# Fetching the condition vector c through the GpSimd queue in a fused adaLN transformer block

## Chip, cores and metric

The kernel runs on one core of a Trainium2 chip. The metric is the device time of one execution in microseconds. Three runs of the kernel before gave 560.43, 561.49 and 562.05 us, a median of 561.49 us.

## What is computed

A transformer block on x of 2048 rows by 512. A condition vector c of 512 numbers is turned into six modulation vectors by one product with w_mod (512 x 3072). The reference, cut to what matters:

```python
x = A_x
mod = (_silu(c) @ w_mod).reshape(c.shape[0], 6, 1, -1)
sa, ca, ga, sb, cb, gb = (mod[:, i] for i in range(6))
h = _layernorm(x) * (1 + ca) + sa
x = x + ga * attention(h)      # 32 heads on 8 kv heads, last 512 keys of the cache
h = _layernorm(x) * (1 + cb) + sb
x = x + gb * mlp(h)            # 512 -> 1792, relu, -> 512
```

Nothing of the attention can start before the first modulation: h needs the shift sa and the scale ca, which need silu(c) and the first third of w_mod (columns 0 to 1023, 1 MB).

## The kernel before

The 2048 rows are four blocks of 512, and each block with each of 32 heads is one unit, 128 in all. For each unit TensorE makes q from the normalised and modulated block (hT) and the head's columns of wq, then scores against the keys, then the product with the values; ScalarE takes the exponential between the two. The output projection and the second half run in the gaps and at the end. All instructions are written in program order into one stream for each engine; a helper (`kb.op`) works out which semaphores each instruction waits for. So the order on an engine is the order in which the build function calls it, and a DMA stands in the stream of the engine that issues it. `dma` takes SyncE unless it is given another engine.

The change touches the start, where the first block is made ready. What happens there, with the lines of the profile:

- Two DMAs bring the first block of x, one half from SyncE, one from ScalarE (L1559). Then c comes as 4 rows of 256 bytes from SyncE (L1560). The modulation weights of sa and ca come in two halves along the contracted dimension, `load_wm01(0)` from SyncE and `load_wm01(1)` from ScalarE (L1561, L1562). After them come wq of heads 0 and 1 from ScalarE, and from SyncE wq of heads 2 and 3, the first keys (a transposing DMA) and the first values. In the profile all plain DMAs carry the line of the helper, L1303, and all transposing ones L1302; one tells them apart by the tile. The weights' tile is called wmw.
- GpSimd makes constants (L1567 to L1575): a tile of ones, the identity matrix by an affine select (L1569), and some memsets.
- TensorE runs 7 products on the tile of ones whose result isn't used (`warm`, L1378, shown as L1371), then turns c into a column by a transpose with the identity (L1415), then 9 more of those products.
- ScalarE takes exp(-c) and a copy of c (L1416, L1417); GpSimd makes silu(c) of them in three steps (L1420 to L1422), the second of which is a power.
- Layer norm of x, four tiles of 128 rows: DVE makes the statistics (L1381, L1382) of tiles 0 to 2, ScalarE those of tile 3. GpSimd takes the power -0.5 of the variances in two steps (L1590), the first for tiles 0 and 1, the second for tiles 2 and 3. DVE normalises tiles 0 to 2 (L1392), and GpSimd tile 3 (L1603).
- TensorE makes the modulation: 32 products of one column each (wmw with silu(c)), 16 with the half that SyncE fetched, then the transposes of tile 0 (L1374), 16 with the other half, and the transposes of tiles 1, 2 and 3. DVE adds the ones for the scale (L1437, modc).
- DVE and ScalarE apply scale and shift to the transposed tiles (L1623 and L1625), half a block at a time, and TensorE makes q of units 0 and 1 from the halves.

The order of TensorE's stream there, as the code has it (L1605 to L1638):

```python
    for f in fs[:len(fs) // 2]:
        f()
    ln_tposes(0, TB[0])
    for f in fs[len(fs) // 2:]:
        f()
    ...
    for tl in range(1, TPB):
        ln_tposes(tl, TB[tl // 2])
    ...
    q_half(0, 0, CC_ORDER, QBK)
```

Of the kernel before, what the change touches and what calls it, by code (L numbers as in the profile page):

```python
# [1198 lines left out]
def build_fast(nc, es, top, A_x, A_k_cache, A_v_cache, A_wq, A_wo, B_x, B_w1, B_w2, c, w_mod, out, flag):  # L1199
    P = 128  # L1200
# [27 lines left out]
    def T(name, shape, dt=BF):  # L1228
        return es.enter_context(nc.sbuf_tensor(name, shape, dt))
# [27 lines left out]
    c_row = T("c_row", [DC, P])  # L1257
# [33 lines left out]
    POOL = kb.stream("pool", sem("s_pool"))  # L1291
    SP = kb.stream("sp", sem("s_sp"))

    def dsem(key):
        if key not in kb.dma_cnt:
            kb.add_dma_sem(key, sem("d_" + key))
        return key

    def dma(out_ap, in_ap, key, reads=(), writes=(), transpose=False, eng=None):
        k = dsem(key)  # L1300
        if transpose:
            return kb.op(SP, lambda e: e.dma_start_transpose(out_ap, in_ap), reads=reads, writes=writes, dma_sem=k)  # L1302
        return kb.op(eng or SP, lambda e: e.dma_start(out_ap, in_ap), reads=reads, writes=writes, dma_sem=k)  # L1303
# [10 lines left out]
    R_ident, R_ones, R_c, R_sc, R_scf, R_tmp, R_cst = (Res(n) for n in ("ident", "ones", "c", "sc", "scf", "tmp", "cst"))  # L1314
# [34 lines left out]
    def load_wm01(i, eng=None):  # L1349
        c0, c1 = i * DC // 2, (i + 1) * DC // 2  # L1350
        dma(wm01[:, c0:c1, :], wm01v[:, c0:c1, :], f"wm{i}", writes=[R_wm[i]], eng=eng)
# [205 lines left out]

    for i in range(2):
        dma(x_sb[:, 2 * i:2 * i + 2, :], xv[:, 2 * i:2 * i + 2, :], f"xa{i}", writes=R_x[2 * i:2 * i + 2], eng=ACT if i else SP)  # L1559
    dma(c_row[:, :], c[0].rearrange("(c p) -> c p", p=P), "c", writes=[R_c])  # L1560
    load_wm01(0)  # L1561
    load_wm01(1, ACT)  # L1562
    load_wq(0, 2, ACT)
# [4 lines left out]
    kb.op(POOL, lambda e: e.memset(cst[:, 0:1], -0.5), writes=[R_cst])  # L1568
    kb.op(POOL, lambda e: e.affine_select(ident[:, :], ones[:, :], pattern=[[1, P]], compare_op=ALU.is_equal, fill=0.0,  # L1569
                                          base=0, channel_multiplier=-1), reads=[R_ones], writes=[R_ident])  # L1570
    kb.op(POOL, lambda e: e.memset(cst[:, 1:2], eps), writes=[R_eps])
    kb.op(POOL, lambda e: e.memset(cst[:, 3:4], -1.0), writes=[R_eps])
    kb.op(POOL, lambda e: e.memset(v_sb[:, :, :, P:VW], 1.0), writes=[R_v1])
# [217 lines left out]
def bass_adaLN_cond__sliding_block_cached__dense_activation_relu__prompt_kernel(  # L1791
# [14 lines left out]
    with ExitStack() as top:  # L1806
        flag = top.enter_context(nc.sbuf_tensor("flag", [1, 8], mybir.dt.int32))
        with ExitStack() as es:
            kb, fast, cut, dma_cnt, flag_ev = build_fast(nc, es, top, *args, flag)
            sems = dict(kb.sems)  # L1810
            meet = top.enter_context(nc.semaphore("s_meet"))
# [71 lines left out]
```

## Time and profile before

| what | us |
|---|---|
| median of three runs | 561.49 |
| the profiled execution, its own time | 560.62 |
| its span, first to last instruction | 558.9 |
| TensorE busy (4060 products) | 549.8 |
| GpSimd busy (53 instructions) | 54.8 |
| c: issue on SyncE, start and duration | 1.24, 0.36 |
| wmw from SyncE: issue to landing | 6.3 |
| wmw from ScalarE: issue to landing | 5.0 |
| TensorE's wait for wmw before its first modulation product | 0.48 |
| TensorE's wait for c | 0.28 |

Times inside the span count from its first instruction. A product's duration is the time of its passage; products follow each other faster than that, so their durations overlap. The engine called POOL in the profile is GpSimd, SP is SyncE, ACT is ScalarE, DVE is VectorE, PE is TensorE and PEld its weight loads. An entry of SPq or ACTq is a DMA being issued. The start, up to the first score product at 12.79 us, is the part in which TensorE is not busy all the time.

### The profile page before, as it was taken

The numbers are of one execution on the slowest core, as the hardware profiler recorded it, in microseconds if no ns is written. First come the engines' busy times: TensorE is split into PE (matmuls) and PEld (weight loads), VectorE is DVE, ScalarE is ACT, GpSimd is POOL, SyncE is SP. The second block draws the span as 40 slices with busy tenths as digits, with TensorE's granted clock in tenths as the row PEclk, the third lists the DMA queues.
The fourth block names the chain that finished last, engine by engine and source line by source line (L and its number), as shares of the span: only waits on it lengthen the run. The fifth ranks groups of instructions, "written<-read, shape, count | busy, mean of one in ns | idle before, by whom it ended". The sixth has DMA issues, their size and how long they took to land.

```text
span 558.9 us, 9664 instructions
## 1 busy us (share of the span) xinstructions
PE 549.8 (98%) x4060; PEld 315.6 (56%) x4134; DVE 252.9 (45%) x549; ACT 349.4 (63%) x453; POOL 54.8 (10%) x53
## 2 busy tenths in 40 slices
PE   8999999999999999999999999999999999999998
PEld 4665555555555555555555555555555654444444
DVE  4455555553546544335445443333354438322134
ACT  5986666666666666666666666666666644432500
POOL 3000022004400000033000000332000000000000
PEclk9999999999999999999999999999999999999999
DMA  9997663522115144352352412111214110200001
GB/s 267 260 206 175 140 154 55 114 42 73 40 38 76 39 79 111 58 133 57 94 95 57 76 39 39 39 39 38 39 39 76 39 30 0 47 30 23 21 30 47
DMA packets 113309, 42.67 MB, mean 76 GB/s; under 512 B 93928, under 2 KB 112104, under 8 KB 113256
## 3 DMA queue, kind: packets, MB, share of 16 engines
q1 hardware_dynamic: 112024, 40.82, 34.4%
q10 hardware_dynamic: 1232, 1.15, 0.6%
q8 instruction: 33, 0.54, 0.4%
q14 instruction: 20, 0.16, 0.1%
HBM read 18.35 MB, written 2.10 MB: 37 GB/s over the span
## 4 chain that ended last, share of the span: by engine, by line
PE 97%; DMA 1%; issue 1%; SPq 0%; ACT 0%; DVE 0%
PE psS L1371 28%; PE psO L1371 27%; PE psQ L1371 23%; PE psW L1371 19%; DMA wmw<-in_w_mod_dram 1%; PE psS L1374 0%; SPq L1303 0%; ACT qT L1484 0%; DVE PT L1713 0%; DVE PT L1715 0%; PE psO L1374 0%
## 5 line engine op out<-in xcount | busy, mean ns | idle before, releaser
L1492 ACT ACTIVATE PT<-psS 128x1024 bf16<-128x1024 f32 x256 | 262.6, 1028 | 127.2 <-PE psS L1371 127.2
L1371 PE MATMUL psS<-qT,kT 128*128 128x512 bf16 x508 | 150.9, 379 | 0.7 <-ACT qT L1484 0.6
L1371 PEld LDWEIGHTS psO<-v,PT 128*128 128x128 bf16 x2048 | 126.6, 98 | 30.2
L1371 PE MATMUL psO<-v,PT 128*128 128x129 bf16 x2048 | 137.0, 220 | 0.0
L1371 PE MATMUL psQ<-hT,wq 128*128 128x512 bf16 (+1 forms) x510 | 130.5, 377 | 0.2
L1502 DVE RECIPROCAL rinv<-psO 128x4 f32<-128x4 f32 x128 | 23.4, 182 | 229.0 <-PE psO L1371 229.0
L1371 PE MATMUL psW<-wo,oT 128*128 128x512 bf16 x454 | 118.1, 379 | 3.0
L1503 DVE TENSOR_TENSOR o<-psO,rinv 128x512 bf16<-128x512 f32 x128 | 88.5, 691 | 4.4
L1371 PEld LDWEIGHTS psQ<-hT,wq 128*128 128x128 bf16 x512 | 50.0, 98 | 60.1 <-ACT qT L1484 0.4
L1371 PEld LDWEIGHTS psS<-qT,kT 128*128 128x128 bf16 x512 | 49.5, 98 | 59.1 <-ACT PT L1492 0.7
L1484 ACT ACTIVATE qT<-psQ 128x512 bf16<-128x512 f32 x127 | 75.2, 592 | 0.8 <-PE psQ L1371 0.8
L1702 ACT ACTIVATE wq<-psS 128x512 bf16<-128x512 f32 x56 | 33.4, 597 | 49.4 <-PE psS L1371 48.9
L1371 PEld LDWEIGHTS psW<-wo,oT 128*128 128x128 bf16 x512 | 45.0, 98 | 32.9 <-DVE acc L1525 1.2
L1525 DVE TENSOR_TENSOR acc<-psW,acc 128x512 f32<-128x512 f32 x48 | 33.2, 692 | 6.7 <-PE psW L1371 6.7
L1371 PE MATMUL psO<-wmw,wq 128*128 128x512 bf16 (+1 forms) x165 | 32.8, 352 | 0.3
L1528 POOL TENSOR_TENSOR acc<-acc,gaf 128x512 f32<-128x512 f32 x12 | 15.6, 1303 | 146.9 <-DVE acc L1525 139.8
L1387 POOL TENSOR_TENSOR rstd<-rstd,cst 128x4 f32<-128x4 f32 x7 | 7.2, 1027 | 216.1 <-DVE rstd L1386 216.1
L1713 DVE TENSOR_TENSOR PT<-psO,gbf 128x512 f32<-128x512 f32 (+1 forms) x12 | 7.5, 624 | 40.4 <-PE psO L1371 40.4
L1371 PE MATMUL psS<-h2T,wmw 128*128 128x512 bf16 x109 | 25.0, 379 | 0.2
L1371 PEld LDWEIGHTS psO<-wmw,wq 128*128 128x128 bf16 x168 | 15.3, 98 | 16.5
L1371 PE MATMUL psS<-hT,wmw 128*128 128x512 bf16 x110 | 24.4, 379 | 0.1
L1381 DVE BATCH_NORM_STATS2 st<-x 128x6 f32<-128x512 bf16 x31 | 21.1, 680 | 4.8 <-DMA x<-in_A_x_dram 4.8
(82 smaller groups left out, 190.9 us busy)
## 6 DMA issues: line engine op xcount, KB each, us to landing
wo<-in_A_wo_dram SPq DMA_DIRECT2D x4, 1024.0 KB, 5.9
wq<-in_A_wq_dram SPq DMA_DIRECT2D x7, 512.0 KB, 5.0
wmw<-in_B_w_dram SPq DMA_DIRECT2D x14, 256.0 KB, 3.1
wmw<-in_w_mod_dram SPq DMA_DIRECT2D x5, 512.0 KB, 5.0
oT<-o SPq DMA_TRANSPOSE x128, 2.4
out_dram<-PT SPq DMA_DIRECT2D x15, 128.0 KB, 1.7
x<-in_A_x_dram SPq DMA_DIRECT2D x3, 512.0 KB, 4.4
v<-in_A_v_cache_dram SPq DMA_DIRECT2D x8, 128.0 KB, 4.1
```

The source lines that it names most:

```text
L1371: kb.op(PE, lambda e: e.matmul(out_ap, lhsT, rhs, start=start, stop=stop), reads=reads, group_writes=[R_b[k] for k in bk], signal=signal)
L1381: kb.op(DVE, lambda e: e.bn_stats(st[:, t, :], x_sb[:, t, :]), reads=[R_x[t]], writes=[R_st[t]])
L1387: kb.op(POOL, lambda e: e.tensor_tensor(rstd[:, sl], rstd[:, sl], cst[:, 0:1].to_broadcast([P, hi - lo]), op=ALU.pow), reads=R_rstd[sl] + ...
L1484: kb.op(ACT, lambda e: e.activation(qT[u % NQT][:, :], bank[bk], ACTF.Copy), reads=[R_b[bk]], writes=[R_qT[u % NQT]])
L1492: kb.op(ACT, lambda e: e.activation(PT[u % NPT][:, pr * 2:pr * 2 + 2, :], s_ps[pr][:, :, :], ACTF.Exp, scale=scale), reads=[R_b[pr * 2], R ...
L1502: kb.op(DVE, lambda e: e.reciprocal(rinv[:, u, :], o_ps[:, :, P]), reads=[R_b[5], R_b[6]], writes=[R_rinv])
L1503: kb.op(DVE, lambda e: e.tensor_tensor(o_sb[u % NOS][:, :, :], o_ps[:, :, 0:P], rinv[:, u, :].unsqueeze(2).to_broadcast([P, TPB, P]), op=A ...
L1525: kb.op(DVE, lambda e: e.tensor_tensor(acc[:, tl, :], bank[WBK], acc[:, tl, :], op=ALU.add), reads=[R_b[WBK], R_acc[tl]], writes=[R_acc[tl]])
L1528: kb.op(eng, lambda e: e.tensor_tensor(acc[:, tl, :], acc[:, tl, :], gaf[:, :], op=ALU.mult), reads=[R_acc[tl], R_ga], writes=[R_acc[tl]])
L1702: kb.op(ACT, lambda e: e.activation(h1T[b % 2][:, fc, :], bank[bk], ACTF.Relu), reads=[R_b[bk]], writes=[R_h1[b % 2][fc]], pre=all_events( ...
L1713: kb.op(DVE, lambda e: e.tensor_tensor(yt[i][:, c0:c1], bank[bk][:, c0:c1], gbf[:, c0:c1], op=ALU.mult), reads=[R_b[bk], R_gb], writes=[R_ ...
```

## The change

The DMA that fetches c is moved from SyncE's stream, where it stood second, to GpSimd's stream, after the affine select that makes the identity and before the memsets of the constants. On SyncE the first half of the modulation weights follows the half of x directly. What c is used for, and all waits on it, are the same.

```diff
     for i in range(2):
         dma(x_sb[:, 2 * i:2 * i + 2, :], xv[:, 2 * i:2 * i + 2, :], f"xa{i}", writes=R_x[2 * i:2 * i + 2], eng=ACT if i else SP)
-    dma(c_row[:, :], c[0].rearrange("(c p) -> c p", p=P), "c", writes=[R_c])
     load_wm01(0)
     load_wm01(1, ACT)
     load_wq(0, 2, ACT)
...
     kb.op(POOL, lambda e: e.memset(cst[:, 0:1], -0.5), writes=[R_cst])
     kb.op(POOL, lambda e: e.affine_select(ident[:, :], ones[:, :], pattern=[[1, P]], compare_op=ALU.is_equal, fill=0.0,
                                           base=0, channel_multiplier=-1), reads=[R_ones], writes=[R_ident])
+    dma(c_row[:, :], c[0].rearrange("(c p) -> c p", p=P), "c", writes=[R_c], eng=POOL)
     kb.op(POOL, lambda e: e.memset(cst[:, 1:2], eps), writes=[R_eps])
     kb.op(POOL, lambda e: e.memset(cst[:, 3:4], -1.0), writes=[R_eps])
     kb.op(POOL, lambda e: e.memset(v_sb[:, :, :, P:VW], 1.0), writes=[R_v1])
```

## The prediction

> **What bounds the kernel now.** I read four views in this order: the page, the chain of waits from 0 to 30 us, the timeline of the first 16 us, and the DMA queues in half-microsecond windows. The page says where a microsecond counts at all:
>
> ```profile
> PE 549.8 (98%) x4060; PEld 315.6 (56%) x4134; DVE 252.9 (45%) x549; ACT 349.4 (63%) x453; POOL 54.8 (10%) x53
> PE 97%; DMA 1%; issue 1%; SPq 0%; ACT 0%; DVE 0%
> PE psS L1371 28%; PE psO L1371 27%; PE psQ L1371 23%; PE psW L1371 19%; DMA wmw<-in_w_mod_dram 1%; PE psS L1374 0%; SPq L1303 0%; ACT qT L1484 0%; DVE PT L1713 0%; DVE PT L1715 0%; PE psO L1374 0%
> ```
>
> TensorE is the bound, and it has no pause worth naming after the start. So the change can only move the start, and what it moves there passes to the end one to one, until TensorE is in its steady loop. The 1% of DMA is one transfer at the start, the first half of the modulation weights (chain of waits):
>
> ```profile
> 1.66 6.31 DMA wmw<-in_w_mod_dram
> 7.97 0.14 issue
> 8.11 0.54 PE psQ L1371 x16
> ```
>
> That transfer is the third that SyncE issues; c is the second. Timeline of the first 16 us (start, duration, engine, line, what; in brackets the idle time before it and who ended that):
>
> ```profile
> 1.23 0.46 ACTq L1303 DMA_DIRECT2D wmw<-in_w_mod_dram  x1
> 1.24 0.36 SPq L1303 DMA_DIRECT2D c_row<-in_c_dram  x1
> 1.32 0.29 POOL L1569 TENSOR_SCALAR_AFFINE_SELECT ident<-ones 128x128 bf16<-128x128 bf16 x1 [0.30 <-POOL cst L1568]
> 1.66 0.41 SPq L1303 DMA_DIRECT2D wmw<-in_w_mod_dram  x1
> 4.49 0.18 PE L1415 MATMUL psO<-ident,c_row 4*128 4x4 bf16 x1 [0.28 <-DMA c_row<-in_c_dram]
> 6.47 0.20 POOL L1422 TENSOR_TENSOR sc_bf<-c_f,tmp 128x4 bf16<-128x4 f32 x1
> 6.79 0.70 POOL L1590 TENSOR_TENSOR rstd<-rstd,cst 128x2 f32<-128x2 f32 x1
> 7.79 0.80 POOL L1590 TENSOR_TENSOR rstd<-rstd,cst 128x2 f32<-128x2 f32 x1 [0.30 <-DVE rstd L1587]
> 8.62 0.41 DVE L1392 TENSOR_SCALAR xn<-x,mv,rstd 128x512 bf16<-128x512 bf16 x1 [0.27 <-POOL rstd L1590]
> 8.69 0.90 POOL L1603 TENSOR_SCALAR xn<-x,s,rstd 128x512 bf16<-128x512 bf16 x1
> 9.65 0.34 PE L1374 MATMUL psS<-ident,xn 128*128 128x128 bf16 x3
> 10.11 0.35 PEld L1371 LDWEIGHTS psQ<-hT,wq 128*128 128x128 bf16 x3 [0.24 <-issue]
> 10.64 0.10 PEld L1371 LDWEIGHTS psQ<-hT,wq 128*128 128x128 bf16 x1 [0.17 <-ACT hT L1625]
> ```
>
> The reader is to see a second path here, which the chain doesn't print because it follows one releaser only. GpSimd makes the last tile of the normalised x (L1603), which ends at 8.69 + 0.90 = 9.59; the transposes of that tile begin on TensorE at 9.65; and they stand on TensorE ahead of the first q product (10.11). This path comes from x through DVE and GpSimd and holds no modulation weight. The two paths meet within half a microsecond.
>
> The queues show why the weights are late (q1 is SyncE's, q10 is ScalarE's; packets, MB, share of 16 engines), first from 4 to 4.5 us, then from 5 to 5.5:
>
> ```profile
> q10 hardware_dynamic: 95, 0.19, 99.5%
> q1 hardware_dynamic: 5, 0.01, 3.4%
> ...
> q1 hardware_dynamic: 73, 0.15, 77.4%
> q10 hardware_dynamic: 25, 0.04, 20.6%
> ```
>
> From 3.5 to 5 us SyncE's queue moves next to nothing while ScalarE's half, issued 0.43 us earlier, has the engines; then they change over. x's two halves, issued at the same 0.79 us, share them evenly. So the order of issue decides the order of transfer, and 0.42 us of issue time can be worth that much or more of landing.
>
> **What the Trainium skill says.** "DMA: Bandwidth & Descriptors", section "SWDGE vs HWDGE vs iDMA": a DMA issued from GpSimd has its descriptors computed by GpSimd's own cores, and its packets go to the same 16 engines, which take turns between its queue and the hardware queues. The trace of before has no such DMA, only q1, q10 and instruction queues, so it can't confirm that. Same page, "Why a DMA increments its semaphore by 16 and not by 1": from GpSimd all 16 engines post the completion whatever the shape, so c, which is 4 rows of 256 bytes, would wait for the slowest engine of a loaded set. "SBUF — State Buffer", section "SBUF: two separate sides": GpSimd can't write descriptors while some DVE operations hold the shared port. The trace rules that out here: DVE's first operation starts at 4.80 us. "TensorE: Matmul & The Clock Gate", Part 1: the array starts at half clock and needs a busy window of about 3.4 us. The trace agrees that there is such a step: the filler products of L1378 follow each other every 0.43 us up to 6.29 and every 0.22 from 6.60.
>
> **The change part by part.** (1) SyncE loses c's issue: 1.66 - 1.24 = 0.42 us. Everything behind it moves up by that: these weights to about 1.24, two wq heads (2.11), the first key transpose (2.62) and value rows (4.49). The weights now start level with ScalarE's half (1.23), so I expect the two halves to share the engines as x's halves do. What gets in ahead of them today is part of ScalarE's wq, which q10 carries beside them from 5.5 us to their end near 6.75: by the windows 0.03 + 0.05 + half of 0.09 = 0.125 MB, at 0.37 MB per us 0.34 us. Bounds for the gain: 0 if SyncE's half still queues behind ScalarE's, 0.5 if both halves (1.05 MB at 0.38 MB/us from 3.5 us, plus the 1.1 us that x's halves take from last byte to landing) land at 7.4. I take 0.34: landing at 7.63, first modulation product at 7.77. ScalarE's half moves from 1.23 + 5.0 = 6.2 to about 7.5, and its products (8.73, then 8.39) still find it. wq, needed at 10.11, shares with the other two heads' wq, which land by 2.11 + 7.2 = 9.3: covered by 0.8 us. The key transpose and value rows are needed after 12.5 and only come earlier.
>
> (2) GpSimd gains one issue between L1569, which ends at 1.61, and the memsets of L1571 to L1575. The queue behind it is five memsets (0.7 us from 1.57 to 2.27), then L1420, which waits for c anyway and runs at 4.98. With 1.0 us for the descriptors (same page, "Latency and other measured facts") the memsets end at 3.3: covered by 1.7 us. The eps column is read by ScalarE at 6.82, the ones of v after 16 us, the zeros and ones of m01 at 9.30.
>
> (3) c lands at another time. Before: used at 4.49. The nearest row is that DMA itself, 3.25 us from issue to use under this load; the page's section on the anatomy of a GpSimd DMA prices the whole at 2.0 us. Lower bound: 1.61 + 2.0 = 3.6, no gain, as the seven filler products hold TensorE to 4.0 and DVE's statistics wait for x until 4.80. Upper bound: 1.61 + 1.0 + (3.25 - 0.36) = 5.5. I take 4.6, a tenth late. That shifts L1420 to L1422 and the first power (L1590, 6.79 to 7.49) by 0.1. The second power starts at 7.79 by DVE's word, 0.30 after the first's end, of which some 0.1 is GpSimd's own step: 0.2 us of delay is free. On TensorE the nine fillers end at 7.63 + 0.1, before 7.77.
>
> (4) What the earlier weights buy. modc (9.30) would start 0.34 earlier, but DVE is in L1392 until 8.62 + 0.41 = 9.03: 0.24 earlier. ScalarE's first shift-and-scale (9.57) and with it its second (L1625) move by that, and the wait of 0.17 us at 10.64 goes. What is late next: the transposes of the last tile stay at 9.65, held by GpSimd's 9.59, so the first q product stays at 10.11 and the fourth can't come before 10.11 + 3 x 0.11 = 10.44. So only 0.17 us comes out at the end; the other 0.17 of the 0.34 is idle time.
>
> Sum: 560.62 (the profiled execution: span 558.9 and 1.7 around it) - 0.17 = 560.45. That execution lies 0.87 below the median of 561.49, so in terms of medians 561.3. A measurement of this kernel can tell some 0.3% (1.7 us) from no change; ten times the gain.
>
> **The rivals.** A: the gain is nothing, 561.5: the halves still run one after the other, or x's path through L1603 is alone decisive. For it: 9.65 follows 9.59 at once. Against it: the 0.17 wait on ScalarE is recorded. B, on the other side: c comes late from GpSimd. Its place is the order on GpSimd: L1420 to L1422 stand ahead of both powers and of L1603, so each 0.1 us of c beyond 4.7 ends at the last tile, its transposes and every q product. Price: landing time less 4.7, less the 0.17 gained. From 4.9 it is a loss, from 6.6 one of over 1.7 us. At the upper bound of 5.5 it gives 561.5 + 0.6 = 562.1. It would pass 6.6 if GpSimd needed preparation for its first DMA: the trace shows 6.1 us of idle "issue" ahead of the all-reduce of gbf (L1449), and with such a pause c would land near 10 and the time be near 566. Against it: the pause ahead of L1569 is only 0.30. A longer wait of TensorE for c could also put off the clock step at 6.3 to 6.6, which costs 0.21 for each of the four fillers after it: 0.8 at most before the real work. C: the whole 0.48 us that TensorE waits for the weights goes (561.0), if L1603 isn't binding; GpSimd's 0.90 us speaks against it.
>
> **How the numbers follow.** My forecast (small gain) 0.55, A 0.20, C 0.03, B below the measurable 0.14, B above it 0.08. None but the last is measurable; noise gives faster 0.03, slower 0.08, same 0.89. The three runs of before spread over 1.6 us; with B's 0.6 on the upper side the range is 559.9 to 563.0.
>
> **What would show it.** SyncE's weights issued at 1.24 and landed near 7.6; q1 and q10 both busy between 4 and 4.5 us; modulation products at 7.8; L1603 still at 8.7 and the last transposes at 9.65; no wait at 10.64; qT's first ACTIVATE 0.17 before 11.84. I am wrong if the product on c starts after 4.9, if GpSimd pauses for microseconds ahead of its DMA, or if L1603 moves.

## The result and the profile after

The changed kernel takes 564.66 us (median of six runs, 564.01 to 564.86); the kernel before took 561.37 us in the same comparison (six runs, 560.43 to 562.05). The ratio is 1.0059, with a 95% interval from 1.0046 to 1.0072. The change costs 3.3 us in this comparison, and the forecast of no measurable change was wrong: the time lies above its range of 559.9 to 563.0.

The profiled execution took 564.17 us with a span of 562.4, 3.5 more than before. The steady part is the same: TensorE is busy for 550.3 us of products (549.8 before). First the changed kernel's page: a new queue, and the line that heads the DMA part of the chain (queue, packets, MB, share of 16 engines; then the chain by line).

```profile
q0 software_dynamic: 32, 0.00, 0.0%
...
PE psS L1371 28%; PE psO L1371 26%; PE psQ L1371 23%; PE psW L1371 20%; DMA c_row<-in_c_dram 1%; ACT qT L1484 0%; DVE hT L1623 0%; DVE PT L1713 0%; DVE PT L1715 0%; POOL ident L1568 0%; PE psS L1374 0%; POOL ones L1566 0%; DVE modc L1437 0%; PE psO L1415 0%; POOL cst L1567 0%
```

Where wmw, the modulation weights, stood in the chain, there is now c itself, all 1 KB of it. The timeline of the changed kernel's first 17 us (start, duration, engine, line, what; in brackets the idle time before it and its releaser):

```profile
1.24 0.46 ACTq L1303 DMA_DIRECT2D wmw<-in_w_mod_dram  x1
1.25 0.42 SPq L1303 DMA_DIRECT2D wmw<-in_w_mod_dram  x1
...
1.59 0.85 POOL L1303 DMA_DIRECT2D c_row<-in_c_dram  x1
...
8.05 0.17 PE L1415 MATMUL psO<-ident,c_row 4*128 4x4 bf16 x1 [3.82 <-DMA c_row<-in_c_dram]
...
8.15 3.80 PE L1371 MATMUL psW<-ones 128*128 128x512 bf16 x9
...
10.02 0.20 POOL L1422 TENSOR_TENSOR sc_bf<-c_f,tmp 128x4 bf16<-128x4 f32 x1
...
10.18 1.51 POOL L1590 TENSOR_TENSOR rstd<-rstd,cst 128x2 f32<-128x2 f32 x2
...
11.79 0.54 PE L1371 MATMUL psQ<-sc_bf,wmw 128*128 128x1 bf16 x16
...
11.80 0.90 POOL L1603 TENSOR_SCALAR xn<-x,s,rstd 128x512 bf16<-128x512 bf16 x1
...
15.52 0.60 ACT L1484 ACTIVATE qT<-psQ 128x512 bf16<-128x512 f32 x1 [0.79 <-PE psQ L1371]
```

The nine filler products and the first qT in the kernel before:

```profile
4.61 3.02 PE L1371 MATMUL psW<-ones 128*128 128x512 bf16 x9
...
11.84 0.60 ACT L1484 ACTIVATE qT<-psQ 128x512 bf16<-128x512 f32 x1 [0.79 <-PE psQ L1371]
```

The reader is to see three things. The weights are issued second, at 1.25 us, as intended; the record of arrivals has them at 1.25 + 6.1 = 7.3 us, before 7.97. But TensorE stands for 3.82 us until c comes, used at 8.05 instead of 4.49. And the nine filler products behind c's transpose take 3.80 us (3.02 before), so that the modulation products behind them on TensorE start only at 11.79 (the last filler's passage ends at 11.95), while silu has been ready since 10.22. The first qT comes 3.68 us later than before (15.52 against 11.84).

The queues of the changed kernel in two windows, 4 to 4.5 us and 5.5 to 6 us:

```profile
q1 hardware_dynamic: 69, 0.14, 72.5%
q10 hardware_dynamic: 34, 0.06, 36.0%
...
q10 hardware_dynamic: 57, 0.12, 59.9%
q1 hardware_dynamic: 56, 0.08, 44.4%
q0 software_dynamic: 8, 0.00, 1.0%
```

SyncE's and ScalarE's halves now share the engines, as foreseen, though not evenly in the first window (0.14 against 0.06 MB). GpSimd had written its descriptors by 1.59 + 0.85 = 2.44 us, but the first packet of its queue q0 runs only after 5.5 us. It then runs while q1 and q10 together still take the engines whole (59.9% and 44.4%): q0 is not held until the other queues are empty.

### The profile page after: what moved, and what is told of

Its sections match the earlier page's. It is cut to its first block, busy times and chain, and to the rows that moved or that the text cites. A ratio compares the mean times of both kernels' runs of the same rounds, so it can differ in the third digit from the quotient of the medians.

```text
span 562.4 us, 9664 instructions
## 1 busy us (share of the span) xinstructions
PE 550.3 (98%) x4060; PEld 315.8 (56%) x4134; DVE 253.0 (45%) x549; ACT 349.3 (62%) x453; POOL 55.7 (10%) x54
## 4 chain that ended last, share of the span: by engine, by line
PE 97%; DMA 1%; issue 1%; DVE 0%; ACT 0%; POOL 0%; POOLq 0%; DVEq 0%
PE psS L1371 28%; PE psO L1371 26%; PE psQ L1371 23%; PE psW L1371 20%; DMA c_row<-in_c_dram 1%; ACT qT L1484 0%; DVE hT L1623 0%; DVE PT L1713 0%; DVE PT L1715 0%; POOL ident L1568 0%; PE psS L1374 0%; POOL ones L1566 0%; DVE modc L1437 0%; PE psO L1415 0%; POOL cst L1567 0%
```

## The experiments

Two theories on why c is late. Q: on the DMA engines it stands behind whatever the hardware queues were handed before it, here the weights. F: a DMA from GpSimd takes 6 us in any case, or the first one does. The first run sets them apart.

**Probes.** Six fetches of c more, from GpSimd into spare tiles, in the kernel before:

```diff
+    probe = lambda i: dma(c_pr[:, i, :], c[0].rearrange("(c p) -> c p", p=P), f"pr{i}", writes=[R_pr_[i]], eng=POOL)
...
     kb.op(POOL, lambda e: e.affine_select(ident[:, :], ones[:, :], pattern=[[1, P]], compare_op=ALU.is_equal, fill=0.0,
                                           base=0, channel_multiplier=-1), reads=[R_ones], writes=[R_ident])
+    for i in range(3):
+        probe(i)
...
+    probe(3)
     TB = [[0, 0, 2, 2], [1, 1, 3, 6]]
...
+    for i in (4, 5):
+        add(90, lambda i=i: probe(i))
```

> The kernel before (c from SyncE) with six more fetches of c from GpSimd into spare tiles that nobody reads: three in a row where the change has its own (about 1.6, 2.5 and 3.3 us), one after L1603 (about 9.7 us), two in the steady loop at unit 90 (near 380 us), where the DMA engines are mostly idle. Theory Q (a GpSimd DMA is served behind what the hardware queues were handed before it): the three early ones land bunched at 7 to 8.5 us whatever their issue time, the one at 9.7 within some 3 to 5 us, the two late ones within 2 to 2.5 us of their issue. Theory F (a GpSimd DMA has a fixed cost of about 6.4 us from issue, load or not): landings at 8.0, 8.9, 9.7 us, and the late ones 6.4 us after issue; a variant, a cost of the first DMA alone, has the first at 8 and the second at well under 6 us from issue. The total stays that of before within 0.3%, since nothing waits.

Measured: 560.61 us (one run), before 560.78. DMA issues of the probe kernel in the windows 1.55 to 1.6, 9.4 to 9.6 and 310 to 312 us (KB each, median us from issue to landing; the unit of the loop was reached at 310, not at the 380 that I had reckoned):

```profile
c_pr<-in_c_dram POOLq DMA_DIRECT2D x1, 1.0 KB, 6.1
...
c_pr<-in_c_dram POOLq DMA_DIRECT2D x1, 1.0 KB, 4.3
...
c_pr<-in_c_dram POOLq DMA_DIRECT2D x2, 1.0 KB, 1.7
```

The same transfer by the same queue takes 6.1 us from the change's place and 1.7 us when the engines are nearly idle. F is out. The variant of F is out too: the second and third in a row needed 5.6 and 6.0. They were not bunched as Q had it: landings at 7.7, 8.1 and 9.0 us by the record of arrivals. What they share is that none of their packets runs before 5.9 us. And the kernel isn't slower: a late GpSimd DMA costs nothing while nobody waits.

**c at the head of GpSimd's stream.**

```diff
+    dma(c_row[:, :], c[0].rearrange("(c p) -> c p", p=P), "c", writes=[R_c], eng=POOL)
     kb.op(POOL, lambda e: e.memset(ones[:, :], 1.0), writes=[R_ones])
...
                                           base=0, channel_multiplier=-1), reads=[R_ones], writes=[R_ident])
-    dma(c_row[:, :], c[0].rearrange("(c p) -> c p", p=P), "c", writes=[R_c], eng=POOL)
```

> The changed kernel with c at the very head of GpSimd's stream (issue near 0.8 us instead of 1.59), ahead of the tile of ones and the identity. Theory Q: descriptors are ready near 1.65 us, before most of the weights are handed over, so c lands 2 us or more earlier than the 8.0 of the change, near 5 to 6, and the loss shrinks to 1 us or less. Theory F: c lands 0.8 us earlier, at 7.2, and the time is 0.8 us below the change's 564.7.

Measured: 563.63 us (562.45 to 564.12), before 560.78, ratio 1.0050 (1.0036 to 1.0065). The issue came at 1.31 us, not 0.80, so it did not get ahead of the weights (1.24, 1.25), and c landed at 7.10. Q's 5 to 6 us is missed. F's numbers, 7.2 us and 0.8 us below the change, came close, but not for F's reason: c is issued only 0.28 us earlier and lands 0.9 us earlier. It even landed a little ahead of the weights that were issued before it (SyncE's half at 1.25 + 6.0 = 7.3), so the line is not a strict one. What TensorE did on c's arrival is of use further down:

```profile
7.15 0.17 PE L1415 MATMUL psO<-ident,c_row 4*128 4x4 bf16 x1 [1.53 <-DMA c_row<-in_c_dram]
...
7.25 2.13 PE L1371 MATMUL psW<-ones 128*128 128x512 bf16 x9
```

**c third on SyncE, no GpSimd DMA.**

```diff
-    dma(c_row[:, :], c[0].rearrange("(c p) -> c p", p=P), "c", writes=[R_c])
     load_wm01(0)
+    dma(c_row[:, :], c[0].rearrange("(c p) -> c p", p=P), "c", writes=[R_c])
     load_wm01(1, ACT)
```

> No GpSimd DMA: c stays on SyncE but is issued after its half of the modulation weights instead of ahead of it. Theory Q, in the form that c's place in the order is what matters: c lands behind the weights at 6.5 to 7.8 us and the time is 1.5 to 3 us above before. Theory F, in the form that only the issuing engine matters: c lands within half a microsecond of before (4.5 to 5.0), and the time is that of before.

Measured: 563.11 us, before 560.78, ratio 1.0037 (1.0022 to 1.0051). This run has the lateness without any GpSimd DMA. From its chain of waits (start, us, what):

```profile
1.24 0.42 SPq L1303
1.66 0.05 issue
1.71 5.28 DMA c_row<-in_c_dram
6.99 0.05 issue
7.03 0.18 PE psO L1415
7.21 3.95 PE psW L1371 x9
```

Put behind the weights, the hardware queue brings c at 6.99; ahead of them, issued 0.47 us earlier, it brought c for 4.49. On one and the same queue, with the same transfers about it, c's place in the order makes it late; GpSimd is not needed for it.

**The weights held back until c has landed.**

```diff
-    load_wm01(0)
-    load_wm01(1, ACT)
...
+    dma(c_row[:, :], c[0].rearrange("(c p) -> c p", p=P), "c", writes=[R_c], eng=POOL)
+    for i in range(2):
+        kb.op(SP, lambda e, i=i: e.dma_start(wm01[:, i * DC // 2:(i + 1) * DC // 2, :], wm01v[:, i * DC // 2:(i + 1) * DC // 2, :]), reads=[R_c], writes=[R_wm[i]], dma_sem=dsem(f"wm{i}"))
+    load_wq(0, 2)
```

> The changed kernel, c from GpSimd at the same place, but the transfers of the weights, wq, keys and values all wait on SyncE until c has landed; only x's two halves are ahead of c on the DMA engines. Theory Q (c is late because of what was handed to the DMA engines before it): c lands at 3.8 to 4.8 us, two to four below the 8.0 of the change. Theory F (GpSimd's first DMA is slow in itself): c lands near 8 again. The time is no measure here: the weights start 3 us late, so it will be 1 to 3 us above before in either case.

Measured: 563.78 us (one run), before 561.00; the time is that of the late weights, behind which TensorE is at half clock as well (four q products take 0.85 us instead of 0.44). The chain of waits has c:

```profile
1.33 0.25 POOL ident L1562
1.59 3.50 DMA c_row<-in_c_dram
5.09 0.02 issue
```

The same GpSimd DMA at the same 1.59 us takes 3.5 us when only x is ahead of it, against 6.4. It lands at 5.09, a little above the expected 4.8: behind x, whose halves land at 4.7 and 4.9. This run takes the weights away altogether. One with c from GpSimd first and the weights right behind it was not made: that its place among the transfers, and not their mere presence, decides for GpSimd's queue too is carried over from SyncE.

**c second on ScalarE.** The change's SyncE part without GpSimd.

```diff
-    dma(c_row[:, :], c[0].rearrange("(c p) -> c p", p=P), "c", writes=[R_c])
+    dma(c_row[:, :], c[0].rearrange("(c p) -> c p", p=P), "c", writes=[R_c], eng=ACT)
```

> SyncE as in the change (weights second), c issued second on ScalarE, ahead of ScalarE's half of the weights. Both theories: c lands near 4.5 as before, SyncE's half of the weights lands at 6.2 to 7.6, ScalarE's half by 8.0. This is what the change set out to do without GpSimd: the wait of 0.17 us at the fourth q product goes, the first qT ACTIVATE comes 0.1 to 0.3 us before the 11.84 of before; total 0.2 us below before, which the runs can't tell from no change.

Measured: 561.92 us (22 runs, 560.56 to 565.71), before 560.78, ratio 1.0024 (1.0014 to 1.0034). A miss. SyncE's weights landed at 6.2 and c in time for 4.77, but ScalarE's half, expected by 8.0, landed at 1.84 + 7.8 = 9.6, and wq moved to the back. The chain of waits:

```profile
1.84 0.41 ACTq L1303
2.25 0.03 issue
2.28 8.86 DMA wq<-in_A_wq_dram
11.14 0.05 issue
11.19 0.68 PE psQ L1371 x4
```

wq, issued at 1.72 before, is now issued at 2.28 and lands at 11.14, and the first q product waits for it at 11.19. What SyncE's half gains here, ScalarE's half and wq lose. This is one execution; why the 22 runs spread over 5 us is not shown.

**c's fetch left out.** Part one of the change alone; the kernel leaves out c and makes the modulation of a constant.

```diff
-    dma(c_row[:, :], c[0].rearrange("(c p) -> c p", p=P), "c", writes=[R_c])
+    kb.op(DVE, lambda e: e.memset(c_row[:, :], 0.5), writes=[R_c])
```

> Part one of the change alone: c's fetch is left out and c_row is filled with a constant by DVE, so no DMA stands ahead of SyncE's half of the weights and nothing waits for c; the modulation is then of another c. Theory as predicted: SyncE's half is issued near 1.24 and lands at 7.2 to 7.7 instead of 7.97, L1603 stays near 8.7, the first qT ACTIVATE comes 0.1 to 0.3 us before the 11.84 of before, total 0.2 us less, not to be told from before. Rival: the earlier half pushes wq back (as wq landed at 11.1 with c second on ScalarE), then the first q product waits for wq and the time is that of before or above.

Measured: 560.39 us, before 561.00, ratio 0.9986 (0.9979 to 0.9993). SyncE's half landed at 7.49, first qT at 11.51 instead of 11.84. Its timeline:

```profile
8.69 0.90 POOL L1603 TENSOR_SCALAR xn<-x,s,rstd 128x512 bf16<-128x512 bf16 x1
...
9.64 0.34 PE L1374 MATMUL psS<-ident,xn 128*128 128x128 bf16 x3 [0.16 <-POOL xn L1603]
...
9.88 0.68 PE L1371 MATMUL psQ<-hT,wq 128*128 128x256 bf16 x4
...
11.51 0.60 ACT L1484 ACTIVATE qT<-psQ 128x512 bf16<-128x512 f32 x1 [0.83 <-PE psQ L1371]
```

L1603 is where it was, and now TensorE is seen to wait for it (0.16). The earlier weights were worth something, and the second path is what caps it.

**How c's lateness reaches the end.** Two theories: G, through GpSimd's order (silu ahead of both powers and L1603); P, through the nine fillers, at half clock. First all fillers ahead of c, then in addition the norm ahead of silu:

```diff
-    warm(7)
-    silu_exp(5)
-    warm(9)
+    warm(16)
+    silu_exp(5)
```

> The changed kernel with all sixteen filler products ahead of c's transpose instead of nine behind it. Theory P (the fillers, at half clock, pass c's lateness on): the modulation products start at 10.3 instead of 11.8 us and the time falls by 1 us or more below the change's 564.7. Theory G (the order on GpSimd passes it on: silu ahead of the powers and L1603): L1603 stays at 11.8 and the time falls by 0.3 us at most. I expect G and P side by side, so a small gain here.

```diff
+    warm(16)
+    silu_exp(5)
...
-    silu_mul()
     ln_stat(0)
...
           reads=[R_x[t3], R_rstd[t3], R_s3], writes=[R_xn[t3]])
+    silu_mul()
     TB = [[0, 0, 2, 2], [1, 1, 3, 6]]
```

> As the kernel with the fillers first, and in addition silu on GpSimd stands behind both powers and L1603, and ScalarE takes tile 3's statistics ahead of exp of c; c still comes from GpSimd and lands late. If P and G are two chains side by side from c: now neither holds, silu is done near 10.2, the modulation products start at 10.3 and the time is 1.2 to 2 us below the change, about 562.9. If one of them alone had been the chain, this brings no more than the fillers first.

(In the second, the four ScalarE instructions L1581 to L1584 also stand ahead of the exp of c.) Measured: 565.12 us, ratio 1.0070 (1.0052 to 1.0088), and 565.53, ratio 1.0080 (1.0062 to 1.0098), before 561.00. Both miss: no gain at all. Products of the kernel with the fillers first:

```profile
8.25 0.17 PE L1415 MATMUL psO<-ident,c_row 4*128 4x4 bf16 x1 [1.97 <-DMA c_row<-in_c_dram]
...
10.48 0.55 PE L1371 MATMUL psQ<-sc_bf,wmw 128*128 128x1 bf16 x16 [2.06 <-POOL sc_bf L1422]
...
13.70 1.06 PE L1371 MATMUL psQ<-hT,wq 128*128 128x256 bf16 x4
...
14.55 1.06 PE L1371 MATMUL psO<-hT,wq 128*128 128x256 bf16 x4
```

The modulation products come at 10.48 instead of 11.79, as P had it, but four q products now follow every 0.85 us; in the changed kernel that was 0.44. With two waits of 2 us and no fillers between, TensorE works at half clock from 11.6 to past 16 us. In the other kernel four q products take 0.85 us at first as well, and silu found GpSimd busy with tile 3's normalisation until 9.70: it was ready at 11.46, 0.7 us later after c's transpose than in the changed kernel. So that run tells nothing on G.

That left the clock. The changed kernel with the wait for c filled:

```diff
-    warm(7)
+    warm(19)
     silu_exp(5)
     warm(9)
```

> The changed kernel with 12 more filler products ahead of c's transpose (19 instead of 7), the nine behind it kept: TensorE no longer stands idle from 4.2 to 8.05 us while c is on its way. Theory H (part of the loss is the clock: the idle wait keeps TensorE at half clock, so the nine fillers behind c take 3.7 us and stand on the path): these nine now take about 2 us, GpSimd's chain (silu, powers, L1603 at 11.8) is the only path, the first qT ACTIVATE comes near 14.6 instead of 15.5 and the time is 0.7 to 1 us below the change. Theory G alone (only GpSimd's order passes the lateness on): no change, 564.4 to 564.8.

Measured: 563.57 us, before 560.60, ratio 1.0054 (1.0039 to 1.0070). To leave out differences between chips, both kernels were measured side by side on one:

> The changed kernel as it is, on the same chip as the next run, so that the clock's share can be read without a change of chip: 3.0 to 3.6 us above before.

> The changed kernel with 12 more fillers ahead of c's transpose once more. Theory H: 0.7 to 1.1 us below the changed kernel of the same call, 2.2 to 2.8 above before. If the clock has no share in the loss: the same time as the changed kernel.

Measured: the changed kernel 564.89 us, ratio 1.0070 (1.0056 to 1.0083), 4.3 us above before; with the gap filled 564.31 (563.24 to 565.00), ratio 1.0053 (1.0038 to 1.0068), 3.7 above; before 560.58. Both lie above what was expected, the medians differ by 0.6 us, and the intervals overlap.

The spans, first to last instruction, are plainer: 562.7 to 563.3 us in the five runs of the changed kernel, 561.5 to 561.7 in the five with the gap filled, medians 563.1 and 561.7 (before 558.8). So the filling takes 1.4 us off a loss of 4.3. In three of the filled runs 2.6 to 3.3 us lie outside the span, in all the others of the two kernels 1.7 to 1.8; what that time is, the traces don't show. The two profiles agree with the spans. First the changed kernel, then the filled one:

```profile
7.99 0.18 PE L1415 MATMUL psO<-ident,c_row 4*128 4x4 bf16 x1 [3.87 <-DMA c_row<-in_c_dram]
...
8.11 4.02 PE L1371 MATMUL psW<-ones 128*128 128x512 bf16 x9
...
11.75 0.90 POOL L1603 TENSOR_SCALAR xn<-x,s,rstd 128x512 bf16<-128x512 bf16 x1
...
16.14 0.60 ACT L1484 ACTIVATE qT<-psQ 128x512 bf16<-128x512 f32 x1 [0.79 <-PE psQ L1371]
```

```profile
7.90 0.17 PE L1415 MATMUL psO<-ident,c_row 4*128 4x4 bf16 x1 [0.44 <-DMA c_row<-in_c_dram]
...
8.00 2.13 PE L1371 MATMUL psW<-ones 128*128 128x512 bf16 x9
...
11.65 0.90 POOL L1603 TENSOR_SCALAR xn<-x,s,rstd 128x512 bf16<-128x512 bf16 x1
...
12.60 0.17 PEld L1374 LDWEIGHTS psS<-ident,xn 128*128 128x128 bf16 x3 [0.30 <-POOL xn L1603]
...
14.58 0.60 ACT L1484 ACTIVATE qT<-psQ 128x512 bf16<-128x512 f32 x1 [0.79 <-PE psQ L1371]
```

With the gap filled the same nine products take 2.13 us, the chain of waits runs from c through silu, the powers and L1603 on GpSimd, and the first qT comes 1.56 us earlier though c is used only 0.09 earlier. In this profile of the changed kernel the half clock outlasts the fillers (seven transposes take 0.91 us, from 13.25, against 0.55), which it did not in the first one: hence 16.14 here and 15.52 there.

The pace of the nine fillers goes with the length of the wait ahead of them. After 0.9 us (the weights held back) and 1.5 us (c at the head of GpSimd) they took 2.13 us, after 2.8 us (c third on SyncE) 4.02, after 3.8 and 3.9 us 3.80 and 4.02. Where between 1.5 and 2.8 us it turns, and whether the length alone decides, no run here shows.

**A version that is faster than both.** In the kernel before, the half that is used first is fetched by ScalarE, whose DMA is ahead:

```diff
-    load_wm01(0)
-    load_wm01(1, ACT)
+    load_wm01(0, ACT)
+    load_wm01(1)
```

> The kernel before with c second on SyncE, but the two halves of the weights exchanged: ScalarE fetches the half that is used first. It lands at 6.2 as ScalarE's did, the other at 8.0, in time for its products near 8.4; wq keeps its place. No GpSimd DMA. As with c's fetch left out, the chain then starts at x and goes through GpSimd's L1603; first qT ACTIVATE near 11.5 instead of 11.84, total 0.3 to 0.6 us below before. If instead the first half's place was not what TensorE waited for, nothing moves.

Measured: 560.07 us (13 runs, 559.88 to 560.47), before 560.60, ratio 0.9990 (0.9982 to 0.9998). First qT at 11.54, as without c's fetch. The 0.5 us of 560 is about what leaving out c's fetch gave (0.6); in both, the chain of waits then starts at x and runs through L1603.

## Why the prediction was wrong

**What held.** Part (1): the weights were issued at 1.25, shared the engines with ScalarE's half, and landed at 7.31 in the changed kernel and at 7.49 without c's fetch, where I had 7.63 with bounds of 7.4 and 7.97 (7.31 is a little under the lower one). Part (2): GpSimd's descriptors took 0.85 us (1.0 taken), nobody waited for the memsets behind them, and there was no pause of microseconds ahead of them. Part (4), the cap by L1603: with c's fetch left out it stays at 8.69 and TensorE waits for it. The size was off: I held the first q product to 10.11 by the transposes, but it most likely waited for DVE's first shift-and-scale (9.59 to 10.00): it started 0.14 us behind that one's end, as it does in the changed kernel, where the chain names DVE. It moved from 10.14 to 9.88, and the gain was 0.33 us, not 0.17. In part (3) the seven fillers held TensorE to 4.21, not to 4.0; nothing hung on that.

**The step that failed is (3), c's landing.** I took 4.6 us with an upper bound of 5.5; it landed at 8.0. The bound was made from c's own row on SyncE, 3.25 us "under this load", plus the time for the descriptors. But that row was measured with c ahead of the weights, and the change puts it behind both halves, 1 MB. The load was the same, the place in it was not. My own reading of the queues, "the order of issue decides the order of transfer", applied to c too, and I used it only for the weights. The runs show it: c landed at 6.99 us behind the weights by SyncE and at 5.09 behind x alone by GpSimd, and took 1.7 us from issue in a quiet stretch. The Trainium skill's price of 2.0 us ("DMA: Bandwidth & Descriptors", section "Anatomy of one DMA — SWDGE (gpsimd) path") agrees with the quiet 1.7 and not with the loaded 6.1. The taking of turns that I quoted from that page doesn't mean a prompt turn: between 2.44 and 5.5 us no packet of q0 ran. What in the DMA engines keeps it waiting is not seen in these traces and stays open.

**Rival B was the right mechanism** and had too small a chance, 0.08, for a loss that can be measured; I had made it depend on a pause for preparation, which didn't occur. Its price, landing less 4.7 less 0.17, gives 8.0 - 4.87 = 3.1 us; the medians moved by 3.3 and the first qT by 3.68. That 3.1 comes so near to 3.3 is in part luck: the price has no clock in it, and in the repeat the medians moved by 4.3. Its path was half right. Where TensorE is at full clock (gap filled, or c at the head of GpSimd), the first qT comes 6.68 us after c's transpose, through silu, the powers and L1603: from 8.05 that is 14.73, or 2.89 us of loss. The changed kernel's 15.52 is 0.79 more, and in the repeat 16.14 was 1.47 more than its 7.99 + 6.68. That rest is the clock, as the filled gap shows: idle from 4.2 to 8.05 us, TensorE runs the nine fillers at half clock (in the repeat also what follows them), and they take the path over from GpSimd. I had put this at 0.8 us at most and as an aside. "TensorE: Matmul & The Clock Gate" (Part 1) has half rate as the default, which sustained work lifts; the trace agrees: the seven fillers ahead of the wait were at half clock, and so were the nine behind it, with 4.02 against 2.13 us.

## What to carry to other kernels

A small transfer that moves to another queue is also moved in the line in front of the DMA engines: price it by what has been issued before its new place, not by its duration at the old one. Before giving a queue a better second place, ask who needs what is pushed back, and in which order; here c was needed before the weights that overtook it. Filler products that stand behind a long wait can become part of the path: here a wait of 2.8 us or more left them at half clock, one of 1.5 us did not.

## What was not expected of the hardware

- A 1 KB DMA from GpSimd took from 1.7 us (engines nearly idle) to 6.4 us (x and the first weights, 1.5 MB, issued ahead of it), and the first of a kernel 0.85 us to issue where the next ones took 0.52.
- At the very head of its stream GpSimd issued c only at 1.31 us, though nothing that the profile shows held it after 0.69.
- A third of what ScalarE's first q operand moved by in the repeat of the change (1.47 of 4.30 us) was the half clock after an idle wait of 3.9 us.
- An idle wait of 1.5 us, after seven fillers at half clock, was followed by fillers at full clock.
